# Linear attention and spectral mixing on one core: the order of the first six output tiles, the queue of the first query load, and three filler matmuls

## The chip, the cores and the metric

The kernel runs on one core of a Trainium2 chip. The metric is the device time of one execution in microseconds (us). "The kernel before" took 421.47 us, the median of three runs (421.24 to 423.12), when the prediction was made. An execution that the profiler recorded has a span some 1.8 us shorter than its time, because the span runs from the first to the last instruction; times of day inside a run are counted from the span's start.

Short names: PE does the matmuls and PEld loads their weights, DVE is the vector engine, ACT the activation engine, POOL issues most loads, SP issues the stores.

## The reference, cut to what matters

```python
# q, k, v: [8, 8, 576, 64]; w_r, w_i: [64, 512, 512]; w_ch: [512, 512]; all float32
phi = lambda t: np.where(t > 0, t, np.exp(t) - 1.0) + 1.0
kv  = einsum('bhsd,bhse->bhde', phi(k), v);  z = phi(k).sum(2)
x   = (phi(q) @ kv) / (phi(q) . z + 1e-6)              # -> [8, 576, 512]
X   = rfft(x, axis=1)[:, :64]                          # 64 modes are kept
Yr  = Xr @ w_r[m] - Xi @ w_i[m];  Yi = Xr @ w_i[m] + Xi @ w_r[m]   # for each mode m
u   = x + irfft(Y, n=576)
out = u + relu(u @ w_ch)
```

The 64 modes have 128 matrices of 512x512, 134 MB in float32. They are loaded once each and used at once; this stream of loads fills the run from about 10 to 384 us.

## The kernel before

Three places matter. First the start: the two halves of the first query block go out one behind the other on SP, and ACT warms up its exponential at once.

```python
    actwarm = const.tile([128, 1], F32, name="actwarm")
    nc.vector.memset(actwarm, 0.0)
    nc.scalar.activation(out=actwarm, in_=actwarm, func=AF.Exp)
    # ... cut ...
            if (nm, b) == ("q", 0):
                for c in range(2):
                    t = sA.tile([128, 2, NJ * Dh], F32, tag="x16", bufs=2, name=f"q32_{c}")
                    pin(nc.sync.dma_start(out=t, in_=rows_in[:, :, c * NJ * Dh : (c + 1) * NJ * Dh]))
```

Second the end of the loads. The last pair of modes has its own code; between mode 62's product and mode 63's stand three matmuls whose result nobody reads ("fillers", there to keep PE busy). Others stand behind the pairs 18 to 30 (`FILL`).

```python
    def keep_warm(n: int):
        for _ in range(n):
            pin(nc.tensor.matmul(last_ps[0], id16, wch16[:, 0, :]))
    # ... cut: last_pair(), after mode 62's product ...
        picks(kk, st, 1)
        pin(nc.vector.tensor_copy(out=Y8[:, :, 0 : NL - 1, :], in_=yt_ps[:, :, 0 : NL - 1, :]))
        keep_warm(3)
        kk = NM - 1                      # mode 63: 8 chunks (dc) of 4 small matmuls (ec)
        for dc in range(NDL):
            for ec in range(NDC):
                pin(nc.tensor.matmul(y_last[:, ec, :], w[:, NDL + dc, ec * 128 : ec * 128 + 128], ...))
    # ... cut ...
    FILL = {**{p: 7 for p in range(18, 27)}, 27: 9, 28: 5, 29: 8, 30: 8}
```

Third the tail. The output is 18 pairs of 128x512 tiles. For each, `channels` puts precomputed sums into PSUM, `rectified` adds the inverse transform of the channel part and applies relu, `finish` adds the inverse of y, adds x on DVE and stores. The first two pairs were summed earlier; tiles of pairs 0 and 1 are finished one by one.

```python
    rectified(1)
    add_inverse(0, 0, (1,))
    channels(2)
    add_one(0, 1)
    rectified(2)
    for i in range(2):
        add_inverse(1, 0, (i,))
        add_one(1, i)
    channels(3)
    rectified(3)
    finish(2)
    for n in range(4, len(pairs)):
        channels(n)
        rectified(n)
        finish(n - 1)
```

## Time and profile before

| what (kernel before, profiled run of 421.32 us) | value |
|---|---|
| span, mean granted clock | 419.6 us, 0.791 |
| DMA share | 9 tenths or more from 10.5 to about 378 us |
| last mode's first weight load / its last four | 386.75 / 387.99 us |
| first addition of line 938 on DVE / last addition | 391.79 / 412.52 us |
| last store issued / end | 413.76 / 419.56 us |

The lines behind the first rows are in the prediction. The tail's own view was read only roughly there, so here is DVE from 391 us on in the kernel before (columns: start, busy us, engine, line, operation, output<-input, shapes, count, then in brackets the idle time before it and what ended it):

```profile
391.79 0.69 DVE L938 TENSOR_TENSOR x_main<-acc,x_main 128x512 f32<-128x512 f32 x1
392.87 1.29 DVE L938 TENSOR_TENSOR x_main<-acc,x_main 128x512 f32<-128x512 f32 x2 [0.39 <-PE acc L737]
394.38 6.10 DVE L810 TENSOR_TENSOR x_main<-acc,x_main 128x1024 f32<-128x1024 f32 x5 [0.22 <-PE acc L737]
...
411.38 1.22 DVE L810 TENSOR_TENSOR x_tail<-acc,x_tail 128x1024 f32<-128x1024 f32 x1
412.52 1.21 DVE L810 TENSOR_TENSOR x_main<-acc,x_main 128x1024 f32<-128x1024 f32 x1
```

Three single additions (line 938), then whole pairs (line 810), back to back to the end. The name `x_tail` marks the two pairs that hold the batches' last rows; its second addition, at 411.38, will matter. The distance that I use below runs from the start of the last four weight loads (387.99) to the start of the last addition (412.52): **24.53 us**. It leaves out everything that the loads decide.

### The profile page before, as it was taken

To read this page: it belongs to the slowest core of one execution; us is meant where nothing else is said; L and a number is where in the kernel's file an instruction comes from. 1 tells how busy PE (TensorE), PEld (TensorE's weight loads), DVE (VectorE), ACT (ScalarE), POOL (GpSimd) and SP (SyncE) were. 2 spreads that over 40 slices of the span, in tenths; PEclk is the share of its full clock that TensorE was granted. 3 is DMA by queue.
4 is the path that set the end of the run, shared out by engine and by line. 5 is a ranking of instruction groups with operands and counts; after the bars stand their busy time and mean duration, and the time that the engine had idled before them with its cause. 6 is when DMAs were issued, how large, how long until landed. Compare 5 with 4: busy or idle time off the path is not lost.

```text
span 419.6 us, 7393 instructions
## 1 busy us (share of the span) xinstructions
PE 289.5 (69%) x3118; PEld 157.0 (37%) x3118; DVE 227.9 (54%) x495; ACT 154.1 (37%) x253; POOL 57.5 (14%) x99
## 2 busy tenths in 40 slices
PE   0359799999607553444343686998798877899992
PEld 0248677787301221222121232433343324364420
DVE  3588979994404462464645353454455433612794
ACT  4677788954101011000000233344253422230782
POOL 4122224210001111111111111111111111130000
PEclk9999958989555555555555589799899989999997
DMA  8999999999999999999999999999999999998698
GB/s 217 211 212 217 209 223 204 227 206 225 216 221 212 215 220 211 219 217 211 223 214 212 223 214 211 223 215 212 221 214 214 219 214 217 219 208 162 229 402 322
DMA packets 16417, 93.17 MB, mean 222 GB/s; under 512 B 2032, under 2 KB 2944, under 8 KB 11968
## 3 DMA queue, kind: packets, MB, share of 16 engines
q0 software_dynamic: 12416, 81.48, 93.3%
q1 hardware_dynamic: 3968, 11.22, 7.1%
q8 instruction: 24, 0.39, 0.3%
q14 instruction: 9, 0.07, 0.0%
HBM read 163.93 MB, written 9.44 MB: 413 GB/s over the span
## 4 chain that ended last, share of the span: by engine, by line
DMA 68%; PE 19%; DVE 4%; issue 3%; POOL 3%; ACT 2%; DVEq 0%; ACTq 0%; POOLq 0%
DMA w<-in_moe_w_i_dram 53%; DMA pick_sb<-row_pick 8%; PE P L431 7%; DMA k<-in_k_dram 7%; PE acc L737 3%; PE acc L776 2%; POOL w L116 2%; PE kvp L256 1%; ACT ke L207 1%; DVE x L292 1%; PE zl L418 1%; PE yt L454 1%; PE xp L322 0%; ACT ys L448 0%; PE num L162 0%
## 5 line engine op out<-in xcount | busy, mean ns | idle before, releaser
L431 PE MATMUL P<-w,xz 128*32 128x512 bf16 x496 | 48.3, 529 | 63.9 <-DMA w<-in_moe_w_i_dram 61.5
L448 ACT CAST ys<-P 128x512 f16<-128x512 f32 x15 | 8.8, 586 | 131.4 <-PE P L431 131.4
L116 POOL DMA_DIRECT2D w<-in_moe_w_r_dram x31 | 17.8, 576 | 244.1 <-PE P L431 240.6
L431 PEld LDWEIGHTS <-xz 128*32 128x32 bf16 x496 | 13.2, 115 | 85.0 <-DMA w<-in_moe_w_i_dram 56.4
L446 DVE CAST ys<-P 128x512 f16<-128x512 f32 x17 | 11.8, 691 | 54.1 <-PE P L431 54.1
L678 PE MATMUL eps<-wch,xTw 128*128 128x512 f16 x144 | 40.6, 409 | 0.0
L162 PEld LDWEIGHTS <-qT 64*128 64x128 f16 (+1 forms) x640 | 22.8, 124 | 31.7 <-issue 17.3
L661 ACT CAST x16w<-x_main 128x512 f16<-128x512 f32 x32 | 19.8, 618 | 37.6 <-DVE x_main L659 37.6
L659 DVE TENSOR_TENSOR x_main<-ya,x_main 128x512 f32<-128x512 f32 x32 | 22.0, 691 | 18.8 <-PE ya L655 18.6
L256 PE MATMUL kvp<-vpad,ke 32*128 32x130 f16 x576 | 23.4, 256 | 8.9 <-ACT qT L243 6.1
L441 DVE COPY xz<-xt_c 64x256 bf16<-64x256 bf16 x62 | 23.0, 370 | 11.5 <-PE P L431 10.7
L686 ACT CAST E<-eps 128x512 f16<-128x512 f32 (+1 forms) x40 | 21.2, 540 | 19.5 <-PE eps L678 19.5
L256 PEld LDWEIGHTS <-ke 32*128 32x128 f16 x576 | 21.5, 113 | 10.6 <-issue 8.5
L162 PE MATMUL nw<-kv,qT 64*128 64x65 f16 (+1 forms) x320 | 18.9, 240 | 9.5 <-DVE x_tail L622 4.5
L418 PE MATMUL zl<-wch,id 128*128 128x512 f16 x96 | 23.1, 380 | 0.0
L292 DVE TENSOR_TENSOR x<-num,rd 128x512 f16<-128x512 f32 x32 | 22.1, 692 | 1.1
L236 PE MATMUL qTp<-id,qe 128*128 128x128 f16 x144 | 14.2, 277 | 12.0 <-DVE qe L220 9.7
L207 ACT ACTIVATE qe<-q 128x1152 f16<-128x1152 f16 (+1 forms) x16 | 17.9, 1157 | 7.6 <-DMA q<-in_q_dram 7.5
L622 DVE TENSOR_TENSOR x_main<-nw,rd 128x256 f32<-128x256 f32 x32 | 11.2, 415 | 17.4 <-PE nw L162 17.4
L670 DVE COPY xTw<-xTp 128x512 f16<-128x512 f16 x36 | 15.0, 416 | 10.0 <-PE xTp L668 9.9
L454 PE MATMUL yt<-pick_sb,ys 128*128 128x32 f16 (+1 forms) x128 | 8.8, 186 | 16.2 <-DMA pick_sb<-row_pick 10.1
L243 ACT COPY qT<-qTp 128x1152 f16<-128x1152 f16 x16 | 19.6, 1289 | 0.4 <-PE qTp L236 0.2
(117 smaller groups left out, 492.9 us busy)
## 6 DMA issues: line engine op xcount, KB each, us to landing
w<-in_moe_w_r_dram POOLq DMA_DIRECT2D x31, 1024.0 KB, 12.5
w<-in_moe_w_i_dram POOLq DMA_DIRECT2D x31, 1024.0 KB, 16.8
out_dram<-x_main SPq DMA_DIRECT2D x10, 512.0 KB, 4.0
k<-in_k_dram POOLq DMA_DIRECT2D x8, 576.0 KB, 12.8
v<-in_v_dram POOLq DMA_DIRECT2D x8, 576.0 KB, 14.2
q<-in_q_dram POOLq DMA_DIRECT2D x7, 576.0 KB, 12.5
out_dram<-x_main SPq DMA_DIRECT2D x2, 1024.0 KB, 4.6
q<-in_q_dram SPq DMA_DIRECT2D x2, 576.0 KB, 4.7
```

What stands on the lines that cost most here:

```text
L116: nc.gpsimd.dma_start(out=w_in[p][half::2], in_=two.rearrange("g (r dc) e -> (g r) dc e", dc=NDW))
L162: mm = nc.tensor.matmul(num[hpo][orow, c0 : c0 + 65], qT[rows, hpp, h2, cols], kv_sb[rows, hpp, h2, :])
L207: pin(nc.scalar.activation(out=ev[:, c], in_=heads(nm, b, c), func=AF.Exp))
L256: nc.tensor.matmul(kv_ps[:, h2, 0:130], phi["k", b][r0 : r0 + 32, j // NJ, j % NJ].rearrange("p o d -> p (o d)"), vp[r0 : r0 + 32, :, j, 0 ...
L292: nc.vector.tensor_tensor(out=dst.rearrange("p (o c d) -> p o c d", o=2, c=4), in0=nv[:, :, :, 0:64], in1=rden.unsqueeze(3).broadcast_to([ ...
L418: pin(nc.tensor.matmul(last_ps[0], id16, wch16[:, 0, :]))
L431: nc.tensor.matmul(P[c : c + n, :], x, w[:, dc, :], start=(dc < NDC), stop=(dc >= n_dc - NDC), tile_position=(0, c), skip_group_check=True,)
L441: pin(nc.vector.tensor_copy(out=xz[p % 2][HALVES[h], :, h, :], in_=src))
L659: pin(nc.vector.tensor_tensor(out=x, in0=acc, in1=x, op=ALU.add))
L661: pin(nc.scalar.copy(out=x16w[t], in_=x))
L678: nc.tensor.matmul(e_ps, xT[:, c, :], wch16[:, c, :], start=(c == 0), stop=(c == NDC - 1))
L686: pin(nc.scalar.copy(out=dst, in_=e_ps[:, cols]))
```

## The change

The intent: get the stream started a little earlier, take PE work off the path behind the last weight, and let the first six tiles be finished and stored one by one, each tile's inverse ahead of the next tile's sums.

```diff
-    nc.scalar.activation(out=actwarm, in_=actwarm, func=AF.Exp)
...
-                for c in range(2):
+                for c, eng in enumerate((nc.sync, nc.scalar)):
-                    pin(nc.sync.dma_start(out=t, ...))
+                    pin(eng.dma_start(out=t, ...))
...
     load(0)
+    nc.scalar.activation(out=actwarm, in_=actwarm, func=AF.Exp)
...
-        keep_warm(3)
         kk = NM - 1
...  (channels takes tiles_of, the tiles of the pair to sum)
+    def sums_of(n: int, i: int):
+        channels(n, (i,))
+        add_inverse(n, 1, (i,))
+        relu(n, i)
...
-    (the tail above, from rectified(1) to the loop over n)
+    for i in range(2):
+        add_inverse(1, 1, (i,))
+        relu(1, i)
+    singles = [(0, 1), (1, 0), (1, 1), (2, 0), (2, 1)]
+    ahead = [(2, 0), (2, 1), (3, 0), (3, 1)]
+    for n, i in singles:
+        add_inverse(n, 0, (i,))
+        if ahead:
+            sums_of(*ahead.pop(0))
+        add_one(n, i)
+    channels(4)
+    rectified(4)
+    finish(3)
+    for n in range(5, len(pairs)):  # as before: channels, rectified, finish of the pair before
```

## The prediction

> **What bounds the kernel now.** I read the page first (share of DMA in the forty slices, then the chain that ended last), then the stretches of time around the two ends of the run, then the single instructions there.
>
> ```profile
> DMA  8999999999999999999999999999999999998698
> DMA 68%; PE 19%; DVE 4%; issue 3%; POOL 3%; ACT 2%; DVEq 0%; ACTq 0%; POOLq 0%
> ```
>
> The DMA digit is 9 from the second slice to the thirty-sixth (10.5 us to 378 us), and 68% of the chain is waiting for transfers. For some 380 us the kernel is a stream of loads and the engines follow. A change can help in three ways only: start the stream earlier, shorten the path from the last weight's landing to the first store, or shorten the tail of stores. The change has one part in each. The stretches (columns: us, busy time of PE, its weight loads, DVE, ACT and POOL, granted clock, DMA share, GB/s):
>
> ```profile
> 2.50:3.00 0.50, 0.00 (x0) 0.00 (x0) 0.00 (x0) 0.00 (x0) 0.50 (x2) 1.00 0.68 184
> 3.00:5.50 2.50, 0.00 (x0) 0.00 (x0) 0.00 (x0) 0.57 (x1) 2.50 (x4) 1.00 1.05 405
> ...
> 384.50:387.50 3.00, 3.00 (x39) 1.22 (x32) 1.32 (x2) 0.00 (x0) 0.00 (x0) 1.00 0.51 94
> 387.50:388.00 0.50, 0.46 (x13) 0.34 (x11) 0.00 (x0) 0.00 (x0) 0.00 (x0) 1.00 0.04 6
> ...
> 398.50:410.75 12.25, 12.25 (x71) 3.10 (x70) 12.14 (x11) 10.80 (x21) 0.00 (x0) 1.00 1.02 403
> 410.75:413.75 3.00, 1.26 (x8) 0.33 (x6) 2.94 (x3) 1.13 (x3) 0.00 (x0) 1.00 0.95 384
> 413.75:417.25 3.50, 0.00 (x0) 0.00 (x0) 0.00 (x0) 0.00 (x0) 0.00 (x0) 0.63 1.06 426
> ```
>
> The reader sees the DMA ramp up only after 2.5 us (0.68 of full for half a microsecond), trickle to an end at about 387.5 us, and then, as stores, run full from 398.5 us. In quarter-microsecond stretches the share falls to 0.73 at 412.0 and to 0.50 at 413.25: late in the tail the stores wait for the engines, so the end is set by the last addition on DVE and the transfer behind it, not by a queue of stores.
>
> At the end of the loads:
>
> ```profile
> 373.51 0.54 POOL L128 DMA_DIRECT2D w<-in_moe_w_i_dram  x1
> DMA to landing us min/median/max: 14.4/14.4/14.4
> 386.08 0.81 PE L418 MATMUL zl<-wch,id 128*128 128x512 f16 x3
> 386.75 1.08 PEld L502 LDWEIGHTS <-w 128*128 128x128 bf16 x28 [0.36 <-issue]
> 387.99 0.17 PEld L502 LDWEIGHTS <-w 128*128 128x128 bf16 x4
> ```
>
> The last piece of the last weight is issued at 373.51 and lands 14.4 us later, at 387.91. The last mode's product (line 502) is 32 small matmuls, four for each of eight chunks. Twenty-eight load weights back to back from 386.75; then there is a hole, and the last four start at 387.99. Those four read the last piece, so they wait for the transfer, though the chain calls that step PE.
>
> **What the Trainium skill says.** "DMA: Bandwidth & Descriptors", section "Issuing engines are not separate DMA queues": transfers issued by SP, ACT and POOL run on the same 16 engines, and issuing from several saves only the sequencer's issue time. The trace agrees as far as it can: the two query issues take 0.43 and 0.45 us on SP, and 0.45 us is the saving. "ScalarE: Activation LUTs", section "What ACT_TABLE_LOAD costs", gives about 1283 ns for a table load; the trace shows 1.28 us here. "TensorE: Matmul & The Clock Gate", section "What's actually happening", says an idle PE falls to half clock after a window of about 3.4 us; here the granted clock is 1.00 from 384 us to 413 us, and taking 0.7 us of fillers out of a busy stretch leaves no such hole. "Perfetto Trace Analysis", section "DMA Optimizations", says splitting transfers lets some start sooner if the DMA engines are idle. In the tail they are idle only for short moments.
>
> **The change part by part.**
>
> *Start.* The second query half is issued on ACT at about 0.74 instead of on SP at about 1.19, and the table load moves behind it: 0.74 + 0.45 + 1.28 + 0.20 (warming exponential) = 2.7 us, still before the first query lands (4.93). Two halves now share the engines, so the first lands later (about 6 instead of 4.9 us) and the second sooner. The exponential of the first keys waits until 9.74 in any case, with ACT idle 2.15 us before it, and the chain goes through the second batch's keys (landing 18.15). So only the ramp counts. If the DMA is full at 2.5 instead of 3.0 us, the stream gains (1 - 0.68) x 0.5 = 0.16 us. Because the loads are the bound up to 384 us, this should carry through. I count -0.15 us, possibly nothing.
>
> *Fillers.* Three filler matmuls behind mode 62 go; PE is spared 0.66 us on the chain. But the pieces land, from their issues plus landing times, at 386.65 (371.75 + 14.9), 387.30 (372.30 + 15.0), 387.64 (372.84 + 14.8) and 387.91. The first product can't begin before 386.65, and it begins at 386.75 now. Without fillers: 16 matmuls at 39 ns from 386.65 end at 387.27, eight from 387.30 to 387.61, four from 387.64 to 387.80, and the last four still wait for 387.91. Gain: 0 us, at most the 0.08 between 387.91 and 387.99.
>
> *Tail.* No work is removed. Pair 2 becomes two single tiles, so DVE does two of 0.69 us, about 0.65 apart, instead of one of 1.22 (+0.07 us), and there is one more store. What moves is the order on PE: the inverse that finishes a tile comes ahead of the next tile's sums. Today DVE waits 0.39 us before the third single tile, 0.22 before pair 2 and about 0.1 before pair 3. In the new order, with 0.215 us per matmul, starting from the inverse of tile 1 at 391.38: the tiles' inverses end at about 391.6, 392.25, 392.9, 393.5 and 394.15, so DVE can add every 0.65 us without a hole and stores come 0.45 to 1.2 us earlier. However, before the inverse of pair 3 the same 19 matmuls stand in both orders (it ends at 395.67 now), and PE has no hole there: pair 3 goes to DVE at about 395.7 both times. From there the order is identical. PE, ACT (0.597 us a relu, two a pair) and DVE all need about 1.2 us a pair, so none has the room to win back time. The early stores save DMA idling at 396 us and turn into longer idling at 412 us. Gain at the end: 0, perhaps 0.05.
>
> Sum: -0.15 + 0 - 0.05, so 421.47 becomes about 421.2 to 421.3. I choose 421.1, as the chunk waits have some slack that I can't see.
>
> **The rivals.** (a) *The fillers are on the path*: the chain lists them with 0.66 us, and if the last piece lands with them out of the way at 387.3, all of that is won: about 420.8. Against it is the hole before the last four weight loads. (b) *The stores are the bound of the tail*: the DMA share is 1.02 from 398.5 to 410.75, and about 10 MB at 403 GB/s is 24.7 us of the 26 us between the first store and the end. Then earlier stores count in full, 0.45 to 0.6 us: about 420.7. Against it are the dips at 412 to 413.75. (c) *Earlier stores collide with the spreading of the last rows*: those two transfers (issued 390.31 and 390.58, landing 3.2 and 3.9 us later, the second at 394.5) gate pair 4's sums, which PE reaches at about 394.6. With two stores 0.45 us earlier in the way they may land a few tenths late: +0.1 to 0.3 us, about 421.6. (d) *A third queue delays the first keys*: there are 2.15 us of slack before it shows; I give it little.
>
> **Range and chances.** If (a) and (b) both hold with the ramp, the sum is -0.15 - 0.66 - 0.5 = -1.3 us: 420.2, my low end. If (c) holds and the ramp gives nothing, 421.7; run to run scatter (421.24 to 423.12 before, two of three within 0.25 us) takes the high end to 421.9. Two per cent is 8.4 us; nothing here is worth a fifth of that. Faster 0.01, same 0.985, slower 0.005.
>
> **What would show it.** Start: DMA share above 0.68 in 2.5 to 3.0 us, and the second keys' landing about 0.15 us sooner. Fillers: weight loads of the last mode starting near 386.6, in groups with holes between, the last four within 0.1 us of the last landing. Tail: single adds 0.65 us apart without holes, pair 3's add about 4.3 us after the inverse of tile 1 as now, deeper dips of the DMA share near 411 to 414. The prediction is wrong if the last piece itself lands earlier by more than 0.3 us, if pair 3's add comes sooner relative to the first store, or if the store stream stays full to the end and stops sooner.

## The result, and the profile after

| | runs (us) | median |
|---|---|---|
| before | 421.24, 421.29, 421.35, 421.47, 422.81, 423.12 | 421.41 |
| changed | 421.71, 421.73, 422.58, 422.68, 423.40, 423.43 | 422.63 |

The ratio is 1.0017 with a 95% interval of 0.9992 to 1.0041: the same at 2%. (A ratio here is the mean time of one kernel's fast runs over that of the other's of the same rounds, so it is not quite the ratio of the medians. All twelve runs count as fast, being within 1.5% of the fastest.) The median lies 0.7 us above the top of my range of 420.2 to 421.9. The runs themselves give two clues. Even the fastest run of the changed kernel is 0.47 us above the fastest of the kernel before; and four of its six runs are 0.87 us or more above its fastest, against two of six.

The profile recorded one of the fast runs, 421.73 us. Its page, the DMA share in slices and the first line of the chain that ended last:

```profile
DMA  8999999999999999999999999999999999997797
DMA 67%; PE 17%; DVE 4%; ACT 3%; issue 3%; POOL 3%; DVEq 0%; ACTq 0%; POOLq 0%
```

The bound is the same stream of loads. The stretches of the changed kernel that answer to those in the prediction (us, busy PE, PEld, DVE, ACT, POOL, granted clock, DMA share, GB/s):

```profile
2.50:3.00 0.50, 0.00 (x0) 0.00 (x0) 0.00 (x0) 0.24 (x2) 0.50 (x2) 1.00 0.70 226
3.00:5.50 2.50, 0.00 (x0) 0.00 (x0) 0.00 (x0) 0.00 (x0) 2.50 (x4) 1.00 1.04 403
...
410.75:413.75 3.00, 1.24 (x8) 0.33 (x6) 2.58 (x3) 1.11 (x3) 0.00 (x0) 1.00 0.93 381
413.75:417.25 3.50, 0.00 (x0) 0.00 (x0) 0.34 (x1) 0.00 (x0) 0.00 (x0) 0.65 1.02 405
```

The ramp is where it was (share 0.70 for 0.68, though 226 GB/s for 184). At the end DVE does 0.36 us less work between 410.75 and 413.75 than before (2.58 for 2.94): something holds it up there. The end of the loads in the changed kernel:

```profile
386.73 1.09 PEld L501 LDWEIGHTS <-w 128*128 128x128 bf16 x28 [0.62 <-issue]
386.76 1.50 PE L501 MATMUL y_last<-xt_c,w 128*128 128x16 bf16 x32 [0.55 <-DMA w<-in_moe_w_i_dram]
387.98 0.17 PEld L501 LDWEIGHTS <-w 128*128 128x128 bf16 x4 [0.15 <-DMA w<-in_moe_w_i_dram]
```

With the fillers gone PE idles 0.55 us for the load and starts the last mode at the same moment as before; the last four weight loads stand at 387.98 for 387.99. Nothing was won there, as predicted. The tail on DVE in the changed kernel:

```profile
391.78 3.28 DVE L938 TENSOR_TENSOR x_main<-acc,x_main 128x512 f32<-128x512 f32 x5
395.69 4.78 DVE L810 TENSOR_TENSOR x_main<-acc,x_main 128x1024 f32<-128x1024 f32 x4 [0.63 <-PE acc L736]
400.52 1.23 DVE L810 TENSOR_TENSOR x_tail<-acc,x_tail 128x1024 f32<-128x1024 f32 x1
401.66 9.66 DVE L810 TENSOR_TENSOR x_main<-acc,x_main 128x1024 f32<-128x1024 f32 x8
411.73 1.22 DVE L810 TENSOR_TENSOR x_tail<-acc,x_tail 128x1024 f32<-128x1024 f32 x1 [0.42 <-ACT acc L786]
412.87 1.21 DVE L810 TENSOR_TENSOR x_main<-acc,x_main 128x1024 f32<-128x1024 f32 x1
```

The five single additions run without a hole, 0.65 us apart; the second hole of 0.22 us becomes one of 0.63 us, and pair 3 comes at 395.69. From there to 410 us the two traces agree to 0.02 us. Then 0.42 us of idling stands in front of the second `x_tail` addition, and the last addition is at 412.87 for 412.52. The distance is 24.90 us for 24.53. The profile puts the idling down to ACT's relu. But the addition waits for the same count of ACT in both programs (250), and in the kernel before that relu ends at 411.54 us, when the addition has been running since 411.38. The addition doesn't need that relu, so the attribution can't be right.

So two things had to be explained: 0.37 us in the tail of every trace of the changed kernel, and runs 1 to 2 us slower than its fastest.

### The profile page after: what moved, and what is told of

Read it like the earlier page. It is cut to its first block, busy times and chain, and to the rows that moved or that the text cites. A ratio compares the mean times of both kernels' runs of the same rounds, so it can differ in the third digit from the quotient of the medians.

```text
span 420.0 us, 7390 instructions
## 1 busy us (share of the span) xinstructions
PE 288.4 (69%) x3115; PEld 156.5 (37%) x3115; DVE 228.5 (54%) x496; ACT 153.9 (37%) x253; POOL 56.4 (13%) x99
## 4 chain that ended last, share of the span: by engine, by line
DMA 67%; PE 17%; DVE 4%; ACT 3%; issue 3%; POOL 3%; DVEq 0%; ACTq 0%; POOLq 0%
DMA w<-in_moe_w_i_dram 52%; DMA pick_sb<-row_pick 8%; PE P L431 7%; DMA k<-in_k_dram 7%; PE acc L736 3%; PE acc L776 2%; POOL w L115 2%; PE eps L677 1%; ACT ke L206 1%; DVE x L291 1%; ACT qT L242 1%; PE kvp L255 1%; PE ya L654 0%; PE xTp L667 0%; PE xp L321 0%
## 5 line engine op out<-in xcount | busy, mean ns | idle before, releaser
L115 POOL DMA_DIRECT2D w<-in_moe_w_r_dram x31 | 16.9, 546 | 245.2 <-PE P L431 240.7
L235 PE MATMUL qTp<-id,qe 128*128 128x128 f16 x144 | 13.2, 265 | 13.0 <-DVE qe L219 10.1
L161 PE MATMUL num<-kv,qT 64*128 64x65 f16 (+1 forms) x320 | 16.4, 217 | 5.2 <-DVE x L291 2.4
```

The lines of the kernel that those rows point to most:

```text
L115: nc.gpsimd.dma_start(out=w_in[p][half::2], in_=two.rearrange("g (r dc) e -> (g r) dc e", dc=NDW))
L161: mm = nc.tensor.matmul(num[hpo][orow, c0 : c0 + 65], qT[rows, hpp, h2, cols], kv_sb[rows, hpp, h2, :])
```

## The experiments

Eighteen kernels ran. The table gives the fastest run, the median, the ratio to the kernel before in the same rounds, and, from the one recorded run, the distance defined above. Runs of the kernel before beside them had medians of 421.24 to 421.41 us.

| run | runs | fastest | median | ratio [95%] | distance |
|---|---|---|---|---|---|
| start_only | 6 | 421.16 | 421.34 | 0.9993 [0.9970, 1.0016] | 24.52 |
| fillers_only | 6 | 421.23 | 422.83 | 1.0019 [0.9988, 1.0049] | 24.54 |
| tail_only | 6 | 421.76 | 422.75 | 1.0023 [0.9995, 1.0050] | 24.89 |
| after_again | 6 | 421.74 | 422.12 | 1.0008 [0.9987, 1.0030] | 24.90 |
| after_plus1 | 6 | 421.02 | 421.91 | 1.0002 [0.9974, 1.0029] | 24.53 |
| before_plus1 | 6 | 421.03 | 421.14 | 0.9987 [0.9962, 1.0012] | 24.91 |
| drop_store | 4 | 421.34 | 422.80 | 1.0023 [0.9984, 1.0061] | 24.53 |
| fill6 | 4 | 421.43 | 421.58 | 0.9994 [0.9960, 1.0028] | 24.55 |
| before_again | 6 | 421.26 | 421.42 | 1.0003 | 24.53 |
| cold | 4 | 421.68 | 423.03 | 1.0026 [1.0008, 1.0044] | 24.55 |
| warm | 6 | 421.34 | 421.40 | 1.0008 | 24.53 |
| after_plus1_warm | 6 | 421.21 | 422.24 | 1.0012 [1.0000, 1.0025] | 25.72 |
| fillers_only_b | 6 | 421.18 | 422.45 | 1.0015 | 25.72 |
| after_fill | 6 | 421.64 | 422.33 | 1.0024 | 24.91 |
| after_fill_plus1 | 6 | 421.28 | 421.29 | 0.9991 [0.9971, 1.0011] | 24.52 |
| after_fill_plus1_y | 6 | 421.32 | 422.47 | 1.0019 [0.9990, 1.0049] | 24.53 |
| after_plus32 | 1 | 422.44 | - | - | 25.72 |
| after_plus64 | 1 | 421.19 | - | - | 24.53 |

### One part at a time

`start_only`, `fillers_only` and `tail_only` are the kernel before with one part of the change (the hunks above); `after_again` is the changed kernel once more.

> Only the first query load is split over two queues, with the table load behind it. Theory A (the stream of loads only starts a little fuller): last weight lands at most 0.15 us earlier, time within 0.3 us of before. Theory B (a third queue delays the first keys and with them everything): first keys' exponential at 9.92 instead of 9.74 us as in the changed kernel, and the whole run 0.2 us or more longer.

> Only the three fillers behind mode 62 go. Theory A (the last weight's landing gates the last mode's product): the last four weight loads of that product stay near 388.0 us, within 0.1 us of before, time unchanged within 0.2 us. Rival (the fillers are on the path): the product ends 0.6 us earlier and the run is 0.6 us shorter.

> Only the tail's order changes, which gives DVE one more instruction ahead of the second tail pair's addition. Theory A (the reorder is free, and the extra instruction puts that addition at a place in DVE's stream where the next instructions must be fetched): pair 3 is added about 395.7 us as before, the addition of the second tail pair starts about 0.35 us late with 0.4 us of idle time before it, and the fast runs are 0.3 to 0.45 us longer than before. Rival (earlier stores are worth their time): 0.3 to 0.5 us shorter. Rival (scatter alone): no idle time there, no difference.

> The changed kernel once more. If its 0.35 us of idle time before the second tail pair's addition belongs to the program, the profile shows it again, and its fastest runs lie 0.3 to 0.45 us above the fastest of before; if it was chance, it is gone. The spread of five more times shows whether the runs at 422.6 and 423.4 are steps that before has too (it has 422.8 and 423.1).

**Measured.** The start alone changes nothing that can be resolved: the second batch's keys come to ACT at 17.88 us, where before has 18.18, the changed kernel 18.24 and its repeat 18.09, so the spread is as large as the gain that I had hoped for, and the ratio is 0.9993. Theory B, which is rival (d) of the prediction, is false: alone, the new start has the first keys' exponential at 9.48 us for 9.74. The tail alone has the 0.37 us: distance 24.89, and its fastest run is 421.76, like the changed kernel's 421.71 and 421.74. The fillers alone leave the distance at 24.54 and the fastest run at 421.23, but four of six runs are 1.3 to 3.2 us above it.

**What follows.** The two losses come from two parts: a fixed one from the tail, and scattered ones at least in part from the fillers. The recorded run of `fillers_only`, 422.52 us, was one of the scattered ones. Its stretches late in the stream of loads:

```profile
350.00:354.00 4.00, 2.54 (x20) 1.61 (x20) 0.69 (x1) 0.84 (x2) 1.09 (x2) 0.65 1.00 213
354.00:358.00 4.00, 3.48 (x12) 1.10 (x9) 2.96 (x6) 0.33 (x1) 0.00 (x0) 0.50 0.94 201
...
366.00:370.00 4.00, 4.00 (x13) 1.25 (x13) 1.35 (x3) 1.74 (x3) 0.00 (x0) 0.50 0.94 201
370.00:374.00 4.00, 4.00 (x36) 2.00 (x36) 0.42 (x1) 0.58 (x1) 1.02 (x2) 0.79 1.02 217
```

The granted clock is 0.50 in two stretches of 6.83 us. In such a stretch a group of nine fillers takes 3.10 us for 2.12 and eight z matmuls 1.99 for 1.14. PE falls behind (it is busy all of 366 to 374), buffers come free late, and the last large load is issued at 372.98 us, where before has 370.13. Its last mode then starts at 388.33. But this stretch lies 15 us ahead of the filler that was removed, so it can't be that filler's doing in the same run. A kernel with the fillers in place, `after_fill_plus1_y` below, has the same two stretches. No slow run of the kernel before was recorded, so that its slow runs have this cause is likely, not shown.

### The 0.37 us of the tail: one instruction more

DVE's program has one addition more in the changed kernel, so everything behind it moves by one place. In the program, counted from 0 with the semaphore instructions and one early branch that the traces leave out, the second `x_tail` addition has place 575 in the kernel before and 576 in the changed one. `after_plus1` and `before_plus1` add one harmless instruction ahead of everything:

```diff
     nc.vector.memset(actwarm, 0.0)
+    nc.vector.memset(actwarm, 0.0)
```

> The changed kernel with one more tiny memset on DVE at the very start, which moves everything behind it by one place in DVE's instruction stream. In the changed kernel the addition of the second tail pair is DVE's instruction 576 = 9 x 64 (counted from 0), here 577. Theory A (a fetch at a multiple of 64 that nothing hides): no idle time before that addition, the last addition ends 0.35 us earlier, fastest runs 421.25 to 421.45 instead of 421.71. Rival (the wait is on ACT or comes of the new order of the tail): the 0.4 us stay, fastest runs 421.7.

> The kernel before with the same extra memset: now its addition of the second tail pair is instruction 576. Theory A: idle time of 0.3 to 0.45 us appears before that addition and the fastest runs go from 421.26 to 421.6 or 421.7, with no other change. Rival (it comes of the new order of the tail): no idle time, fastest runs 421.3.

**Measured.** DVE at the end of the tail, first `after_plus1`, then `before_plus1`:

```profile
407.37 3.65 DVE L811 TENSOR_TENSOR x_main<-acc,x_main 128x1024 f32<-128x1024 f32 x3
411.08 1.23 DVE L811 TENSOR_TENSOR x_tail<-acc,x_tail 128x1024 f32<-128x1024 f32 x1
412.22 1.22 DVE L811 TENSOR_TENSOR x_main<-acc,x_main 128x1024 f32<-128x1024 f32 x1
```

```profile
407.44 3.66 DVE L811 TENSOR_TENSOR x_main<-acc,x_main 128x1024 f32<-128x1024 f32 x3
411.51 1.23 DVE L811 TENSOR_TENSOR x_tail<-acc,x_tail 128x1024 f32<-128x1024 f32 x1 [0.42 <-ACT acc L787]
412.66 1.21 DVE L811 TENSOR_TENSOR x_main<-acc,x_main 128x1024 f32<-128x1024 f32 x1
```

One instruction more takes the hole out of the new tail (24.53 us) and puts it into the old one (24.91 us). The new order therefore costs nothing and wins nothing: 24.53 us either way. The hole belongs to where this addition stands in DVE's program. (In the kernel before, place 576 holds the last addition, with no hole ahead of it.) The totals follow for `after_plus1`, whose fastest run is 421.02. They do not for `before_plus1`: it has the hole, and yet its fastest run is 421.03 and its median 421.14, the lowest of all. In its recorded run the last four weight loads stand at 387.75, 0.24 us earlier than before, and the last store needs 5.41 us for 5.79; together that is more than the hole. Why, I don't know, and at these intervals the ratio of 0.9987 [0.9962, 1.0012] does not show it to be faster.

### Are the stores the bound? And what do fillers cost?

`drop_store` leaves out the stores of pairs 4 and 5 (1 MB, so the output is wrong); `fill6` puts six fillers where the kernel before has three.

```diff
+        if n in (4, 5):
+            return
         store(t0, 2)
```

```diff
-        keep_warm(3)
+        keep_warm(6)
```

> The kernel before without the stores of pairs 4 and 5 (1 MB, its rows of the output are wrong on purpose). Theory A (the tail's end is set by the last additions and the transfer behind them): fast runs within 0.2 us of before. Rival (the stream of stores is the bound): 1 MB at some 403 GB/s less, 2.6 us shorter.

> The kernel before with six fillers behind mode 62 instead of three. Theory A (the last piece lands at 387.9 and three fillers fit ahead of it): three more take 0.65 us of PE; the 32 small products then start near 387.4 without a hole and take about 1.07 us for 28, so their end moves from 388.3 to about 388.6: fast runs 0.2 to 0.4 us longer than before, not 0.65. Rival (the fillers are on the path): 0.65 us longer.

**Measured.** The stretches of `drop_store` in the tail:

```profile
398.50:402.00 3.50, 3.50 (x22) 0.83 (x19) 3.42 (x4) 2.96 (x7) 0.00 (x0) 1.00 0.37 151
402.00:405.50 3.50, 3.50 (x19) 0.78 (x18) 3.50 (x4) 3.12 (x7) 0.00 (x0) 1.00 1.01 390
405.50:410.75 5.25, 5.25 (x31) 1.43 (x30) 5.22 (x5) 4.72 (x9) 0.00 (x0) 1.00 0.97 384
410.75:413.75 3.00, 1.20 (x8) 0.33 (x6) 2.89 (x3) 1.07 (x3) 0.00 (x0) 1.00 0.94 378
```

The DMA share falls to 0.37 while the two stores are missing, but the engines' work is the same in each stretch, the last store goes out at 413.71 us (413.76 before), and the end stays at 419.6. A megabyte less changes nothing, so earlier stores could not help: rival (b) is false, and the additions set the end. In `fill6` the weight loads of the last mode and the fillers ahead of them are:

```profile
386.09 1.46 PE L418 MATMUL zl<-wch,id 128*128 128x512 f16 x6
386.27 0.62 DVE L495 CAST Y<-yt 128x448 f16<-128x448 f32 x1 [0.51 <-PE yt L454]
387.17 1.17 PEld L502 LDWEIGHTS <-w 128*128 128x128 bf16 x32
```

Three more fillers take 0.65 us more, but the mode starts 0.42 us later and now runs without its hole: the last four loads stand at 388.15, only 0.16 us later, and the two fastest runs are 0.2 us above those of the kernel before (421.43 and 421.44 for about 421.2). Fillers in front of a wait for a load cost only what reaches past the landing. So rival (a) is false too.

### What makes the slow runs

The suspicion was that the clock falls where PE has holes. `cold` takes the fillers behind pairs 27 to 29 away, `warm` adds some around pair 27, `after_plus1_warm` adds them to `after_plus1`, and `before_again` is the kernel before.

```diff
-    FILL = {**{p: 7 for p in range(18, 27)}, 27: 9, 28: 5, 29: 8, 30: 8}
+    FILL = {**{p: 7 for p in range(18, 27)}, 30: 8}                          # cold
+    FILL = {**{p: 7 for p in range(18, 27)}, 27: 12, 28: 5, 29: 8, 30: 8}    # warm
+        keep_warm(3 if p == 27 else 0)      # warm: twice more inside pair 27
```

> The kernel before, unchanged, against itself: shows what the comparison says of two equal programs. Theory A (times come in steps, a group at 421.2 to 421.5 and slower ones at 422.5 and more, for every kernel): both groups appear, medians of six can differ by over 1 us. Rival (the slower runs belong to the changed kernel): all but one of the six under 421.6.

> The kernel before without its fillers behind mode pairs 27, 28 and 29 (22 matmuls), so that PE idles more between 350 and 375 us. Theory A (the slower runs are those in which the granted clock falls to half in 350 to 375 us): the clock falls there in every run, the product of pair 30 starts late. Without 22 fillers PE has up to 4.7 us less to do, so if half clock takes no more than it saves, the time stays near 421.3; if PE falls behind, 422.5 or more in most runs. Rival (the slower runs come from the transfers): share of slower runs as before, one in three.

> The kernel before with three fillers in each of the two holes of 0.7 and 0.8 us behind pair 27's product and three more behind that pair. Theory A: the clock stays at 1.00 in 350 to 375 us, and at most one of six runs is over 422. Rival (the clock's fall has nothing to do with these holes, or the slower runs nothing with the clock): a third to a half of the runs over 422 as before.

> The changed kernel with the extra memset and the fillers of the run warm. Theory A: no idle time before the second tail pair's addition, no slower runs: median 421.0 to 421.3, below both kernels by 0.1 to 0.3 us against the fast group of before. Rival: slower runs as often as in the changed kernel, median above 421.6.

**Measured.** `cold` does what was feared. Its stretches:

```profile
354.00:358.00 4.00, 0.62 (x3) 0.11 (x1) 2.53 (x5) 0.00 (x0) 0.00 (x0) 0.99 0.92 197
358.00:362.00 4.00, 3.33 (x23) 1.15 (x25) 1.35 (x2) 0.00 (x0) 1.09 (x2) 0.50 1.08 229
...
370.00:374.00 4.00, 4.00 (x25) 1.23 (x25) 0.91 (x3) 1.17 (x2) 0.00 (x0) 0.50 1.02 217
```

PE is busy for 0.62 of 4 us, then the clock is at half for 17 us, the last large load goes out at 374.59 us, where before has 370.13, and the median is 423.03 us. `warm` was a miss: four of its six runs lie within 0.1 us, but two are 1.3 and 1.6 us slower, about as with the kernel before. Half a clock alone isn't yet a loss: the recorded runs of `before_again` and `start_only` have it from about 352 to 359 us and took 421.50 and 421.16. It costs where PE no longer catches up before the end of the loads.

The surprise was `after_plus1_warm`. It was meant to be the best version; its runs are 421.21, 421.68, and four of 422.1 to 422.4. Its recorded run (422.40) shows where that comes from (stretches at the end of the loads; the first is the place of the removed fillers):

```profile
386.10:386.85 0.75, 0.19 (x5) 0.12 (x6) 0.54 (x1) 0.00 (x0) 0.00 (x0) 1.00 0.48 85
388.00:389.60 1.60, 1.23 (x16) 1.04 (x16) 0.52 (x2) 0.44 (x2) 0.00 (x0) 1.00 0.00 0
389.60:393.05 3.45, 3.42 (x11) 1.23 (x9) 1.51 (x3) 2.24 (x5) 0.56 (x1) 0.51 0.35 93
393.05:396.00 2.95, 2.95 (x16) 1.32 (x14) 2.87 (x5) 2.41 (x5) 0.00 (x0) 1.00 0.98 326
```

PE is busy for 0.19 us of the 0.75 in which the fillers used to stand, and in the window from 389.60 to 393.01 the clock is at half, exactly where PE's chain of matmuls leads to the first additions. The distance is 25.72 us: 1.19 us more.

### Do the fillers behind mode 62 prevent that?

`fillers_only_b` repeats `fillers_only`. `after_fill` is the changed kernel with the three fillers put back; `after_fill_plus1` has one memset more; `after_fill_plus1_y` has one filler more behind the last mode.

```diff
+        keep_warm(3)                                 # after_fill, ahead of kk = NM - 1
+    nc.vector.memset(actwarm, 0.0)                   # after_fill_plus1, as well
+        keep_warm(1)                                 # ..._y, behind the last copy from y_last
```

> The kernel before without the three fillers behind mode 62, a second time. Theory A (without them PE idles about 0.55 us while it waits for the last pieces, so in some runs the granted clock falls to half for one stretch of 3.4 us near 389 to 393 us): half of the runs or more lie over 0.3 us above the fastest group, before about one in four; if the profiled run is such a one, its clock is 0.50 there. Rival (the larger share of slower runs was chance): one or two of six.

> The changed kernel with the three fillers put back: new start and new tail alone. Theory A: fastest group 421.7 as in the changed kernel (DVE's instruction 576 is still the second tail pair's addition: 24.90 us from the last chunk's products to the last addition), but one or two slower runs of six, so a median of 421.7 to 421.9. Rival (fillers don't matter): three or four slower runs of six, median over 422.

> The same with the extra memset on DVE. Theory A: both costs gone: 24.53 us from the last chunk's products to the last addition, fastest group 421.0 to 421.3, one or two slower of six, median at or just below that of before. Rival: median over 421.6.

> The same with one more filler in the hole of 0.3 us behind the last mode's product, where PE waits for DVE's copy. Theory A: no later than the run without it (the filler takes 0.22 us of 0.3), slower runs no more often. Rival: the filler delays the transposes, 0.1 us longer.

**Measured.** `fillers_only_b`, a kernel that differs from the kernel before in nothing but the three fillers, has the same fall in its recorded run: half clock from 389.66 to 393.08, distance 25.72, 422.74 us. Five of its six runs are over 1.2 us above its fastest. With the fillers back, no recorded run has the fall. `after_fill_plus1` has four of six runs between 421.28 and 421.30, a median of 421.29. `after_fill` was a miss in its total: I expected few slow runs, and its recorded run was slow through an early half-clock stretch (351.45 to 361.69 us), as was that of `after_fill_plus1_y` (351.9 to 358.7 and 365.6 to 372.4). `after_fill_plus1_y` missed as well: three of its six runs were 2 us and more above its fastest, though its filler leaves the distance at 24.53. Six runs are too few to compare such shares kernel by kernel.

What the recorded runs do allow is a comparison by phase. In all twenty traces the clock changes only at the edges of windows of 3.41 us, and where these edges fall differs from run to run. The window that would have to fall begins at an edge between 386.2 and 389.7:

| traces without the fillers (edge, us) | clock at half behind the edge? |
|---|---|
| after_plus32 389.39, after_plus1_warm 389.60, fillers_only_b 389.66 | yes, all three |
| after_plus1 387.01, after_plus64 387.01, after_again 387.09, after 387.47, fillers_only 388.78 (late run) | no, all five |

| traces with the fillers, edge in the same place | |
|---|---|
| start_only 389.61, fill6 389.71 | no |

A window that ends between 389.4 and 389.7 holds all the holes from 386 to 389.6: the one of the fillers (0.55 us), the one before the last piece, and the one behind the product (0.32 us); in `fillers_only_b`, all but 0.10 us of them. An edge at 387 or 388 divides them. In the window ahead of the edge PE idled 0.93, 0.91 and 0.82 us in the three traces that fell; in the others without the fillers no window here has more than 0.65. With the fillers in place the first hole is closed, and the same window passes: `start_only` has PE busy for all of 386.10 to 386.85, and idle for 0.37 us in the whole window.

```profile
386.10:386.85 0.75, 0.75 (x14) 0.41 (x13) 0.58 (x1) 0.00 (x0) 0.00 (x0) 1.00 0.49 85
389.60:393.05 3.45, 3.18 (x15) 1.43 (x14) 2.46 (x4) 2.74 (x7) 0.57 (x1) 1.00 0.50 143
```

So removing the fillers brings the fall, at some places of the edge. But the sum of idle time is not the whole rule. Elsewhere windows with far more of it stay at full clock. In the kernel before, between two edges, PE is busy for only 1.61 of 3.41 us, and the next window is at full clock all the same:

```profile
288.38:291.79 3.41, 1.61 (x22) 0.50 (x20) 0.29 (x1) 0.34 (x2) 0.00 (x0) 1.00 1.02 216
291.79:295.20 3.41, 3.41 (x27) 1.70 (x26) 1.77 (x4) 2.23 (x4) 1.08 (x2) 1.00 0.99 211
```

And `fillers_only` falls at 364.88 us behind a window with 0.52 us of idle time. One rival is left untested: the windows that fell at 389.4 to 389.7 also hold the last mode's 32 matmuls of 16 columns, so what PE does while busy may count as well as how long it idles.

The unrecorded runs agree. Sorted by their excess over the fastest run of the same kernel, 13 of the 36 timed runs without the fillers lie 0.8 to 1.3 us above it, the size of this fall; of the kernel before none of 50, and of the ten other kernels with the fillers (`cold` left out) one of 56. (I chose that bin after seeing the 1.19 us, and its upper edge matters: up to 1.6 us it is 14 of 36 against 6 of 50 and 4 of 56, which is still a clear difference.) Larger excesses, over 1.3 us, come to all: 9 of 36, 14 of 50, 14 of 56.

### Is it every 64th place?

576 is nine times 64. If the hole came with every multiple of 64, then place 640 should have it, and 608 not. Both kernels are the changed one with 32 or 64 memsets more.

```diff
     nc.vector.memset(actwarm, 0.0)
+    nc.vector.memset(actwarm, 0.0)   # 32 (after_plus32) or 64 (after_plus64) of them
```

> The changed kernel with 32 extra memsets on DVE at the start, where DVE waits until 6 us anyway: the second tail pair's addition is instruction 608 = 9.5 x 64. Theory (multiples of 64): no idle time before it, 24.53 us from the last chunk's products to the last addition. Rival (multiples of 32): 0.4 us of idle time, 24.90.

> The same with 64 extra memsets: instruction 640 = 10 x 64. Theory (multiples of 64, and rival 32 too): 0.4 us of idle time, 24.90 us. Rival (only place 576 of this program): none, 24.53.

**Measured.** The end of DVE's tail in `after_plus64`:

```profile
411.38 1.23 DVE L874 TENSOR_TENSOR x_tail<-acc,x_tail 128x1024 f32<-128x1024 f32 x1
412.52 1.21 DVE L874 TENSOR_TENSOR x_main<-acc,x_main 128x1024 f32<-128x1024 f32 x1
```

There is no hole at place 640 (distance 24.53), nor at 608 (the 25.72 of `after_plus32` is 24.53 plus the 1.19 of the clock, its window from 389.39 on being at half). "Every multiple of 64" is false. What stands is narrower: the hole appeared in all five traces in which the addition has place 576 (`after`, `after_again`, `tail_only`, `before_plus1`, `after_fill`), and in none of the fifteen in which it has 575, 577, 608 or 640. In the five, the semaphore instruction just ahead of the addition is recorded at the usual moment (411.30 us in `after`), and the addition follows it 0.42 to 0.44 us later in place of 0.07. A refill of the instruction stream would fit such a fixed place. The traces do record transfers of instructions. In queue q14 they are nine packets of 8192 bytes a run, of which five come earlier when 32 or 64 memsets are added and so belong to DVE. These five start when DVE has begun roughly 60, 195, 310, 450 and 575 instructions, with the added memsets counted as well, so they are some 130 places apart and would spare 608 and 640. The last one starts at 413.8 us in `before` and `after`, behind the addition, but at 403.1 us in `after_plus1`, so it shifts just where the addition goes from place 576 to 577. Yet none ends inside the hole. The cause of the hole stays open; that it goes with the place, not with the order of the tiles, is shown.

## Why the prediction was wrong

The point was 421.1 and the median came out at 422.63. By the prediction's own steps:

**The bound: right.** The page after shows the same stream of loads, and no part of the change touches it.

**Start, "-0.15 us, possibly nothing": possibly nothing.** The DMA share from 2.5 to 3.0 us was 0.70 and not 1.0. `start_only` has the ratio 0.9993 with an interval from 0.9970 to 1.0016, which is 1.9 us wide. The term is not shown, and 0.15 us was below what this comparison could have shown.

**Fillers, "Gain: 0 us": right for the path, and wrong in what it left out.** The last piece's landing was the gate: 387.98 after, 387.99 before, and three fillers more moved it by only 0.16 us. (The "groups with holes between" didn't show: 28 weight loads ran back to back from 386.73.) The failed step is in the part on the clock: "taking 0.7 us of fillers out of a busy stretch leaves no such hole." I compared a hole of 0.7 us with a window of 3.4 us and took the matter as closed. But in three of eight recorded runs without the fillers, and in none of twelve with them, the clock fell to half behind a window that held the hole of 0.55 us (0.45 of it in one of them) and the shorter ones behind it; that cost 1.19 us each time. What exactly the clock counts stays open. The fall is probably the larger part of the miss, but no slow run of the changed kernel itself was recorded: both of its traces are of fast runs without the fall, and that its slow runs have it is inferred from their excess. I had written down what the fillers cost and not what they were for.

**Tail, "Gain at the end: 0, perhaps 0.05": right in the mechanism, wrong in one term.** The singles came 0.65 us apart without holes and pair 3 at 395.69, "about 395.7 both times", and from there the order was the same; with one memset more the distance is 24.53 us in both orders. The mis-sized term is "(+0.07 us)" for one more instruction on DVE: it cost 0.37 us, at the other end of the tail and through the place of an addition in the program, which no view had shown me and which I could not have added up from durations.

**Range: too narrow.** "Run to run scatter ... two of three within 0.25 us" took the high end to 421.9. Three runs don't show how often a run is slow: over all rounds 14 of 50 runs of the kernel before lie more than 1.3 us above the fastest of their round, and with the fall behind the last mode added, 22 of 36 without fillers lie at least 0.8 us above theirs. A median of few runs then falls easily on a slow one. The range should have reached 423.4, which runs of the kernel before reached as well.

**Rivals.** (a), fillers on the path, and (b), stores as the bound, are refuted by `fill6` and `drop_store`. (c), a collision with the transfers of the last rows, did not show: the additions from pair 3 up to 410 us stand within 0.02 us of before. (d), delayed first keys, is refuted by `start_only` (9.48 us for 9.74). What happened was none of the rivals. Adding up: 421.3 for a fast run of the kernel before, 0.37 for the place in the program, and 1.19 for the clock in some runs give 421.7 and 422.9; the six runs measured are 421.7 twice, 422.6 and 422.7, which is 0.2 to 0.3 below the sum, and 423.4 twice, with more than these two causes explain. Luck had a part too: `after_again`, the same program, had a median of 422.12.

**Did any version beat both?** Not by what was run. `after_fill_plus1`, the change with its fillers back and one memset more, has the median 421.29 for 421.26 beside it; `before_plus1` 421.14 for 421.24. Both intervals hold 1.

## What to carry to other kernels

Before taking filler work off an engine whose clock depends on how busy it is, look at the clock of many runs, not of one: whether the window fell went with where its edges lay, and neither the largest hole nor the sum of the holes foretold it everywhere. A cost on the path of zero is not the whole cost. When a tail is a chain of back-to-back instructions, a single added or removed instruction can cost more than its own duration, so try the same program shifted by one before crediting or blaming a reordering. And look at the distribution of many runs before choosing a range: if a third of the runs are over a microsecond slow, the median moves with the luck of the draw.

## What the Trainium skill lacked or had wrong

- "TensorE: Matmul & The Clock Gate", section "HAM oscillation — how this bites in real kernels", gives as the rule to have no PE idle gaps longer than about 3.4 us. Here a window fell with a largest single hole of 0.56 us and two shorter ones in it (three of eight traces without the fillers, none of twelve with them; 1.19 us lost each time). The section "A second HAM failure mode: psum-queue depth-cycling" of the same page does say that frequent short idling makes the clock swing, but gives no sum of idle time at which it happens; these runs don't fix one either, since a window with 1.80 us of idle time stayed at full clock (kernel before, 288.38 to 291.79 us).
- The same page, section "What's actually happening", has the window of 3413 ns, free-running, and a clock that is either full or half. All traces agree: half-clock stretches of 3.41, 6.83, 10.24 and 17.07 us, with edges at a different place in each run. It draws the consequence for the warm-up at a kernel's start, but lacks the one for a fall later on: of the runs without the fillers those fell whose edge lay at 389.4 to 389.7 us, and those with an edge at 387.0 to 388.8 us did not.
- "Runtime: NRT & Kernel Launch", section "Instruction fetch mechanics", describes the refill of an engine's instructions in 16 KiB blocks of 256 and calls the cost of crossing a boundary mostly hidden. It doesn't say when the place of an instruction shows. Here DVE's recorded refills are packets of 8192 bytes some 130 places apart, and an addition at place 576 started 0.42 to 0.44 us behind the semaphore instruction ahead of it in place of 0.07, in five of five traces; at places 575, 577, 608 and 640 in none of fifteen. That the two belong together is not shown. The profile's attribution of that idle time to ACT was wrong.
